# Products and ScalarE copies in place of VectorE transposes in the doubling inverse of a DeltaNet kernel

## Chip, cores and metric

The kernel runs on one core of one Trainium2 chip. The metric is the device time of one execution in microseconds. Each instruction goes to one of five engines: TensorE (PE; its weight loads are listed as PEld), VectorE (DVE), ScalarE (ACT), GpSimd (POOL) and SyncE (SP). Every engine takes its instructions in the order in which the program lists them. DMAs are issued here from SP's and ScalarE's queues, and a few at the start from GpSimd's.

## The reference

```python
q, k, v: (4, 8, 768, 48); beta: (4, 8, 768)           # float32
k_n = k / (norm(k) + 1e-06)
for t in range(768):
    y[:, :, t] = einsum('bhd,bhde->bhe', q[:, :, t], state)
    v_old = einsum('bhde,bhd->bhe', state, k_n[:, :, t])
    state += beta[:, :, t] * einsum('bhd,bhe->bhde', k_n[:, :, t], v[:, :, t] - v_old)
x = y as (3072, 384)
h = x @ w_in                                           # (3072, 2048)
out = (h * cos(h)) @ w_out                             # (3072, 384)
```

A delta-rule recurrence over 768 steps for 32 heads (4 batches, 8 heads), and behind it a feed-forward block whose activation is h cos h.

## The kernel before, in words

**The recurrence in chunks.** The 768 steps are cut into 24 units of C = 32 steps (`unit(n)`). For a unit, `turn` and `turn_out` put keys and queries with the head dimension on partitions, `gram` makes the products of keys with keys and queries, `gram_keys` scales the first, `gram_queries` masks the second. The unit's triangular system needs the inverse of a unit lower triangular 32x32 matrix for each of 32 heads. Then `state`, `right`, `solve`, `solve_out`, `update`, `update_out`, `within` and `features` go through the recurrence: `update_out(n)` changes the state that `state(n+1)` reads, so these are a chain from unit to unit. `features_out` writes the unit's share of the feed-forward input, `x_ffn`.

**Three ways to the inverse.** From unit 4 on the inverse is made on GpSimd by substitution (`invert`, lines 856 and 863), between two trips through DRAM (`gram_put`, `gram_get`, `put`, `get`). Units 2 and 3 (pair 1) invert halves of 16, partly on VectorE (tasks `inv 1 x`), and put them together with `solve_half`, `half_out`, `between`, `between_out`. Units 0 and 1 are inverted by doubling, without DRAM, and this is what is changed.

**Doubling.** `double_first` masks the scaled gram (line 691) and transposes it (701). `double_rest` builds identity minus the masked matrix (706) and masks the block off the diagonal (691 again). Then six levels follow, each for both head parities (`par`) and both units, 24 tasks `("double", n, level, par)`:

```python
LEVELS = [
    (LEFT, TURNED, 1), (SQUARE, SUM, 2), (LEFT, TURNED, 2),
    (SQUARE, SUM, 1), (OFF, TURNED, 1), (LEFT, SUM, 1),
]
```

An entry names the tile that is loaded as weights, the first tile that streams, and how many tiles stream side by side. Line 736 issues eight matmuls per task. Results are taken from PSUM by a ScalarE copy (744), a VectorE transpose (752), and a VectorE addition (756). At levels 0, 1 and 2 a transpose of the product is needed, at level 3 one of the sum (749).

**Norms.** `norms_square` (ScalarE, 554) and `norms_sum` (VectorE, 559) give the squared norm of the keys, `norms_root` (GpSimd, 571) its root. `scale` runs five small VectorE operations: plus 1e-6 (582), square (584), reciprocal (585), times beta (587), spread (590). It runs 14 times in all, four of them for units 0 to 3.

**Weights.** w_in and w_out arrive as 28 pieces in a wider format. Each piece goes through `narrow_load` (DMA), `narrow_split` on ScalarE (lines 525 and 529), `narrow_shift` on VectorE (533) and `narrow_add` on GpSimd (537). `hidden(p, f)` for k-th quarter of columns needs the pieces up to 3(k + 1); the output products need the pieces from 12 on.

**Feed-forward.** The first two pairs of units use plain products (`hidden`, line 1076; the very first also plain `output`, 1274), later ones products with fewer multiplications (`layer`, 1250; `product`, 1332), with sums of inputs and results on VectorE and GpSimd.

**Order.** `add(key, engine, cost, emit, deps, ...)` lists a task with what it depends on. The tasks are numbered in the order of these calls, and `Order.LINE` gives the order in which they are emitted, found beforehand and written out as numbers. `Order.OTHER` lists the tasks that take their second choice: DMAs on ScalarE's queue in place of SP's, sums on GpSimd in place of VectorE or the other way round. Among the tasks are 56 calls of `keep_warm`, placed by `LINE` like the others: a matmul of 128x256 on a constant tile (line 492, two rows in the profile), which nobody reads. A call emits nothing once the first output product has been emitted.

Of the kernel before, what the change touches and what calls it, by code (L numbers as in the profile page):

```python
# [59 lines left out]
class Order:  # L60

    OTHER = {
        ('gram_put', 2), ('q', 3), ('gram_get', 1), ('inv', 1, 0), ('put', 1), ('gram_put',
        4), ('gram_put', 5), ('v', 7), ('v', 8), ('v', 9), ('blocks', 11, 1), ('gram_put',
        11), ('put', 5), ('v', 13), ('put', 6), ('gram_put', 15), ('gram_get', 7), ('get',
        15), ('v', 16), ('blocks', 16, 0), ('blocks', 16, 1), ('gram_put', 16), ('blocks',
        18, 1), ('k', 19), ('blocks', 19, 0), ('gram_get', 9), ('get', 19), ('gram_put',
        20), ('v', 21), ('gram_put', 21), ('put', 10), ('gram_put', 22), ('v', 23),
        ('gram_put', 23), ('gram_get', 11), ('right', 4, 4), ('left', 1, 1, 0), ('left', 1,
        3, 0), ('left', 1, 3, 1), ('store', 1, 0), ('x_sum', 2, 'd'), ('x_sum', 2, 'n'),  # L70
        ('x_sum', 2, 'm'), ('x_sum', 2, 'e'), ('x_sum', 2, 'k'), ('x_sum', 2, 'g'),
        ('x_sum', 2, 'i'), ('x_sum', 2, 'l'), ('x_sum', 2, 'f'), ('x_sum', 2, 'b0'),
        ('left', 2, 4, 1), ('left', 2, 3, 1), ('x_sum', 3, 'd'), ('x_sum', 3, 'n'),
        ('x_sum', 3, 'm'), ('x_sum', 3, 'e'), ('x_sum', 3, 'k'), ('x_sum', 3, 'g'),
        ('x_sum', 3, 'i'), ('x_sum', 3, 'l'), ('x_sum', 3, 'h'), ('x_sum', 3, 'b0'),
        ('left', 3, 4, 1), ('left', 3, 3, 1), ('x_sum', 4, 'd'), ('x_sum', 4, 'm'),
        ('x_sum', 4, 'g'), ('x_sum', 4, 'i'), ('left', 4, 3, 0), ('left', 4, 3, 1),
        ('store', 4, 0), ('x_sum', 5, 'd'), ('x_sum', 5, 'e'), ('x_sum', 5, 'l'), ('x_sum',
        5, 'h'), ('x_sum', 5, 'b0'), ('left', 5, 2, 0), ('left', 5, 4, 1), ('left', 5, 3,
        0), ('left', 5, 3, 1), ('store', 5, 0), ('x_sum', 6, 'd'), ('x_sum', 6, 'g'),  # L80
        ('x_sum', 6, 'l'), ('x_sum', 6, 'f'), ('x_sum', 6, 'b0'), ('left', 6, 1, 0),
        ('left', 6, 4, 0), ('store', 6, 1), ('x_sum', 7, 'd'), ('x_sum', 7, 'm'), ('x_sum',
        7, 'g'), ('x_sum', 7, 'i'), ('x_sum', 7, 'f'), ('x_sum', 7, 'h'), ('x_sum', 7,
        'b0'), ('left', 7, 4, 0), ('left', 7, 4, 1), ('left', 7, 3, 1), ('x_sum', 8, 'd'),
        ('x_sum', 8, 'm'), ('x_sum', 8, 'e'), ('x_sum', 8, 'k'), ('x_sum', 8, 'g'),
        ('x_sum', 8, 'l'), ('left', 8, 3, 0), ('store', 8, 0), ('store', 8, 1), ('x_sum', 9,
        'd'), ('x_sum', 9, 'm'), ('x_sum', 9, 'e'), ('x_sum', 9, 'k'), ('x_sum', 9, 'i'),
        ('x_sum', 9, 'l'), ('x_sum', 9, 'b0'), ('left', 9, 1, 0), ('left', 9, 2, 0),
        ('left', 9, 1, 1), ('left', 9, 3, 0), ('store', 9, 0), ('x_sum', 10, 'k'), ('x_sum',
        10, 'i'), ('x_sum', 10, 'l'), ('x_sum', 10, 'h'), ('x_sum', 10, 'b0'), ('left', 10,  # L90
        1, 0), ('left', 10, 1, 1), ('left', 10, 4, 1), ('left', 10, 3, 0), ('left', 10, 3,
        1), ('store', 10, 0), ('x_sum', 11, 'd'), ('x_sum', 11, 'e'), ('x_sum', 11, 'k'),
        ('x_sum', 11, 'g'), ('x_sum', 11, 'f'), ('left', 11, 1, 0), ('left', 11, 2, 0),
        ('left', 11, 1, 1), ('left', 11, 3, 0), ('left', 11, 3, 1), ('store', 11, 1),
        ('store_right', 11), ('weights', 5), ('weights', 7), ('weights', 15), ('weights',
        16), ('weights', 18), ('weights', 20), ('weights', 22), ('weights', 23), ('weights',
        25), ('weights', 27)
# [142 lines left out]
def kernel(  # L240
# [84 lines left out]
    def half(i):  # L325
        return slice(DP * i, DP * i + DP)
# [1599 lines left out]
```

## Time and profile before

| | us |
|---|---|
| median of 3 runs | 639.41 (638.9 to 640.19) |
| the profiled execution | 643.63 |
| its span, first to last instruction | 641.8 |
| granted TensorE clock, mean | 0.992 |

The profile is of one execution. Its page lists for each engine the busy time, the share of the span and the instructions, and then the span in 40 slices of 16 us, where a digit is the busy share in tenths; PEclk is the clock that TensorE was granted. A granted clock below 1 makes matmuls longer. The trace behind the page answers for a stretch: the busy time of each engine in it, the instructions in order of time with what ended the idle time before them, and the chain of waits, which goes back from the last instruction to whatever released it.

The work of units 0 and 1 lies in the first 75 us. Some starting points: the first `turn` product at 6.78, the first `gram` at 10.29, the first doubling product at 15.06, `solve` of unit 0 at 48.48, the first `hidden` product at 60.43, `solve` of unit 1 at 65.44.

### The profile page before, as it was taken

To read this page: it belongs to the slowest core of one execution; us is meant where nothing else is said; L and a number is where in the kernel's file an instruction comes from. 1 tells how busy PE (TensorE), PEld (TensorE's weight loads), DVE (VectorE), ACT (ScalarE), POOL (GpSimd) and SP (SyncE) were. 2 spreads that over 40 slices of the span, in tenths; PEclk is the share of its full clock that TensorE was granted. 3 is DMA by queue.
4 is the path that set the end of the run, shared out by engine and by line. 5 is a ranking of instruction groups with operands and counts; after the bars stand their busy time and mean duration, and the time that the engine had idled before them with its cause. 6 is when DMAs were issued, how large, how long until landed. Compare 5 with 4: busy or idle time off the path is not lost.

```text
span 641.8 us, 24181 instructions
## 1 busy us (share of the span) xinstructions
PE 621.0 (97%) x10176; PEld 577.7 (90%) x10176; DVE 495.8 (77%) x1025; ACT 297.6 (46%) x528; POOL 435.2 (68%) x780
## 2 busy tenths in 40 slices
PE   5999989999999999999999999999999999999997
PEld 4867877997899999999999999999999999999997
DVE  5786746788899999887888898888888786656682
ACT  3447645563334454643642544643643553545440
POOL 5337787778778788888789887886883883112231
PEclk9899989999999999999999999999999999999999
DMA  9869565563551454435436235243304102000000
GB/s 186 213 141 236 103 163 121 117 119 54 101 81 22 92 91 70 88 69 83 79 64 103 49 68 101 51 65 66 72 4 82 41 2 42 19 2 26 1 25 25
DMA packets 209380, 50.36 MB, mean 78 GB/s; under 512 B 200920, under 2 KB 204280, under 8 KB 209272
## 3 DMA queue, kind: packets, MB, share of 16 engines
q1 hardware_dynamic: 161896, 35.03, 29.2%
q10 hardware_dynamic: 47072, 13.25, 9.9%
q8 instruction: 80, 1.31, 0.8%
q0 software_dynamic: 304, 0.54, 0.4%
q14 instruction: 28, 0.23, 0.1%
HBM read 38.55 MB, written 10.22 MB: 76 GB/s over the span
## 4 chain that ended last, share of the span: by engine, by line
PE 88%; DVE 5%; DMA 3%; issue 1%; ACT 1%; SPq 0%; POOL 0%; ACTq 0%; DVEq 0%
PE p_out L1332 28%; PE p_h L1250 27%; PE p_h L1076 7%; PE p_kq L907 4%; PE p_out L1274 3%; PE p_s L1004 3%; PE p_g L652 3%; PE p_kq L1034 3%; PE p_u L979 2%; PE p_h L736 2%; PE p_out L492 2%; PE p_h L1332 2%; PE p_z L1055 1%; DMA kp<-in_k_dram 1%; DMA out_dram<-o 1%
## 5 line engine op out<-in xcount | busy, mean ns | idle before, releaser
L856 POOL TENSOR_TENSOR part<-z,gb 128x126 f32<-128x126 f32 (+23 forms) x321 | 142.5, 444 | 42.8 <-DMA gb<-g_dr 13.7
L863 POOL TENSOR_TENSOR z<-z,part 128x126 f32<-128x126 f32 (+23 forms) x321 | 146.0, 455 | 25.2
L1332 PE MATMUL p_out<-w_out,g_ffn 128*128 128x192 f32 x672 | 121.8, 328 | 1.3 <-ACT o L1371 0.7
L1332 PEld LDWEIGHTS p_out<-w_out,g_ffn 128*128 128x128 f32 x672 | 107.7, 190 | 2.5 <-ACT o L1371 0.8
L1129 ACT ACTIVATE turns<-turns,halfpi 128x512 f32<-128x512 f32 x96 | 68.0, 719 | 55.7 <-DVE turns L1120 43.0
L1332 PE MATMUL p_out<-w_sum,g_ffn 128*128 128x192 f32 x496 | 89.7, 329 | 0.2 <-DVE o L1384 0.2
L1250 PE MATMUL p_h<-x_sum,w_in 128*128 128x128 f32 x640 | 84.0, 277 | 0.0
L1332 PEld LDWEIGHTS p_out<-w_sum,g_ffn 128*128 128x128 f32 x496 | 79.6, 190 | 1.2 <-issue 0.4
L1113 ACT ACTIVATE turns<-g_ffn,quarter_turn 128x512 int32<-128x512 f32 x70 | 49.8, 719 | 66.1 <-DVE g_ffn L1267 23.5
L1250 PEld LDWEIGHTS p_h<-x_sum,w_in 128*128 128x128 f32 x640 | 78.8, 192 | 1.2
L1267 DVE TENSOR_TENSOR g_ffn<-g_ffn,p_h 128x512 f32<-128x512 f32 x80 | 54.2, 680 | 16.1 <-PE p_h L1250 15.4
L1120 DVE SCALAR_TENSOR_TENSOR turns<-g_ffn,turns 128x512 f32<-128x512 f32 x70 | 55.2, 795 | 13.2 <-ACT turns L1113 13.0
L1047 ACT COPY y<-p_kq 32x384 f32<-32x384 f32 x96 | 45.2, 470 | 34.1 <-PE p_kq L1034 25.3
L1132 DVE TENSOR_TENSOR g_ffn<-turns,g_ffn 128x512 f32<-128x512 f32 x70 | 51.9, 750 | 4.1 <-ACT turns L1129 4.0
L1250 PE MATMUL p_h<-x_sum,in_sum 128*128 128x128 f32 x400 | 53.0, 277 | 0.4 <-DVE g_ffn L1267 0.4
L571 POOL TENSOR_TENSOR knrm<-ksum,halves 128x16 f32<-128x16 f32 (+1 forms) x14 | 36.3, 2596 | 24.9 <-DVE ksum L559 24.9
L1250 PEld LDWEIGHTS p_h<-x_sum,in_sum 128*128 128x128 f32 x400 | 49.6, 192 | 1.5 <-DVE g_ffn L1267 0.7
L1384 DVE SCALAR_TENSOR_TENSOR o<-p_out,o 128x192 f32<-128x192 f32 x74 | 25.1, 351 | 29.5 <-PE p_out L1332 28.4
L1076 PE MATMUL p_h<-x_ffn,w_in 128*128 128x128 f32 x384 | 47.4, 283 | 0.0
L1076 PEld LDWEIGHTS p_h<-x_ffn,w_in 128*128 128x128 f32 x384 | 45.7, 198 | 1.2
L1250 PE MATMUL p_h<-x_ffn,w_in 128*128 128x128 f32 x320 | 42.4, 277 | 0.0
L1348 POOL TENSOR_TENSOR g_ffn<-g_ffn,g_ffn 128x512 f32<-128x512 f32 x18 | 25.8, 1442 | 23.1 <-PE p_out L1332 19.3
(163 smaller groups left out, 1072.1 us busy)
## 6 DMA issues: line engine op xcount, KB each, us to landing
g_ffn<-in_moe_w_in_dram SPq DMA_DIRECT2D x10, 512.0 KB
gb<-g_dr SPq DMA_DIRECT2D x14, 256.0 KB
vp<-in_v_dram SPq DMA_DIRECT2D x68, 48.0 KB
g_ffn<-in_moe_w_out_dram SPq DMA_DIRECT2D x8, 384.0 KB
g_ffn<-in_moe_w_out_dram ACTq DMA_DIRECT2D x8, 384.0 KB
kp<-in_k_dram SPq DMA_DIRECT2D x120, 24.0 KB
out_dram<-o SPq DMA_DIRECT2D x14, 192.0 KB
zt<-z_dr SPq DMA_DIRECT2D x72, 32.0 KB
```

What stands on the lines that cost most here:

```text
L571: nc.gpsimd.tensor_tensor(out=scales[m][2][:, part], in0=sums[m, part.start][:, 0:n], in1=halves[:, 0:n], op=ALU.pow,)
L856: eng.tensor_tensor(out=part, in0=z[:, 0:rows, j, None].to_broadcast(shape), in1=a[:, j, None, j + 1 :].to_broadcast(shape), op=ALU.mult,)
L863: eng.tensor_tensor(out=behind, in0=behind, in1=part, op=ALU.subtract)
L1047: nc.scalar.copy(by_parity(y[quarter(b)]), p_kq[quarter(b ^ 1), :, b % 2])
L1076: nc.tensor.matmul(p_h[:, i], w_in[:, t, (4 * k + i) * 128 : (4 * k + i + 1) * 128], xts[p][:, t, unit * 128 : (unit + 1) * 128], start=(i ...
L1113: nc.scalar.activation(turns[p, f], hidden_of(p, f), AF.Identity, bias=quarter_turn, scale=TURN)
L1120: nc.vector.scalar_tensor_tensor(out=r, in0=hidden_of(p, f), scalar=TURN, in1=t, op0=ALU.mult, op1=ALU.subtract,)
L1129: nc.scalar.activation(r, r, AF.Sin, bias=halfpi, scale=2.0 * math.pi)
L1132: nc.vector.tensor_tensor(out=place(p, f), in0=step_of(rests.pop((p, f)), f), in1=step_of(hidden_of(p, f), f), op=ALU.mult,)
L1250: nc.tensor.matmul(p_h[:, e], in_block(*w)[:, e], x_of(p, b), start=new and e == 0, stop=True, skip_group_check=True,)
L1267: nc.vector.tensor_tensor(out=part_of(p, to), in0=part_of(p, one), in1=part_of(p, two), op=op)
L1332: nc.tensor.matmul(p_o, left(p, part, a)[:, e % 4], right(e, b), start=(e == 0), stop=(e == FT // 2 - 1), skip_group_check=True,)
```

## The change

The `scale` of the norms is split: 1e-6 and the square go to two ScalarE activations with a bias tile (`norms_near`, a task `near` of its own between `norms` and `scale`). The off-diagonal mask becomes a GpSimd task `double_off`, which level 4 waits for. Level 0 makes the product and, by exchanging the two operands, its transpose; level 2 does the same with its first half. The transposes of levels 0 and 2 become ScalarE copies; that of level 1 stays.

```diff
-    tiny = const.tile([128, 2, H], FP, name="tiny")
+    tiny = const.tile([128, 1], FP, name="tiny")
...
+    def norms_near(m, part):
+        knrm = scales[m][2][:, part]
+        krec = krecs[m, part.start] = work.tile([128, 2, H], FP, name="krec")[
+            :, 0 : part.stop - part.start
+        ]
+        nc.scalar.activation(krec, knrm, AF.Square, bias=tiny)
+        nc.scalar.activation(knrm, knrm, AF.Identity, bias=tiny)
...
     def scale(m, part):
-        nc.vector.tensor_tensor(out=knrm, in0=knrm, in1=tiny[:, 0:n], op=ALU.add)
-        krec = work.tile([128, 2, H], FP, name="krec")[:, 0:n]
-        nc.vector.tensor_tensor(out=krec, in0=knrm, in1=knrm, op=ALU.mult)
+        krec = krecs.pop((m, part.start))
         nc.vector.reciprocal(krec, krec)
...
-        masked(n, OFF, far_block)
+    def double_off(n):
+        masked(n, OFF, far_block, nc.gpsimd)
...
     LEVELS = [
-        (LEFT, TURNED, 1), (SQUARE, SUM, 2), (LEFT, TURNED, 2),
-        (SQUARE, SUM, 1), (OFF, TURNED, 1), (LEFT, SUM, 1),
+        [(LEFT, TURNED, 1, 0), (TURNED, LEFT, 1, 1)], [(SQUARE, SUM, 2, 0)],
+        [(TURNED, LEFT, 1, 0), (LEFT, SUM, 1, 1)], [(SQUARE, SUM, 1, 0)],
+        [(OFF, TURNED, 1, 0)], [(LEFT, SUM, 1, 0)],
     ]
-    TURNS = {0: (SQUARE, 0), 1: (LEFT, 1), 2: (SQUARE, 0)}
+    TURNS = {0: (SQUARE, 1), 1: (LEFT, 1), 2: (SQUARE, 0)}
...
-            nc.vector.transpose(m[:, to, par], p_ds[n, par][:, at])
+            if level == 1:
+                nc.vector.transpose(m[:, to, par], p_ds[n, par][:, at])
+            else:
+                nc.scalar.copy(m[:, to, par], p_ds[n, par][:, at])
...
+        add(("double_off", n), "POOL", 1.1, lambda: double_off(n), [("double_first", n)])
...
-                deps = last[par] + ([("double_rest", n)] if level == 1 else [])
+                deps = last[par] + {1: [("double_rest", n)], 4: [("double_off", n)]}.get(level, [])
...
+            add(("near", m, a), "ACT", 0.5, lambda: norms_near(m, part), [("norms", m, a)])
```

`LINE` and `OTHER` are new as well. On TensorE, by tasks (W3 stands for three calls of `keep_warm`; `double n level par`; the other numbers are the unit, or pair and column group):

```
before  turn 0, W2, gram 0, turn 1, double 0 0 1, 0 0 0, gram 1, W1, double 0 1 0, 1 0 0, W2,
        double 0 1 1, 1 1 0, W3, 0 2 0, W2, 0 2 1, 1 0 1, turn 2, W2, double 1 1 1, turn 3,
        double 0 3 0, 0 3 1, W1, gram 2, W1, double 1 2 0, W2, 0 4 1, W2, gram 3, double 0 4 0, W2,
        1 2 1, 0 5 0, 0 5 1, turn 4, W1, solve 0
after   turn 0, W2, gram 0, W1, turn 1, double 0 0 1, 0 0 0, gram 1, W3, double 0 1 1, 0 1 0, W1,
        1 0 0, 0 2 1, turn 2, W2, double 0 3 1, turn 3, double 1 0 1, 0 2 0, 1 1 0, gram 2, W4,
        double 0 3 0, W2, 0 4 1, 1 1 1, W1, 0 4 0, gram 3, double 0 5 1, 0 5 0, W3, turn 4,
        double 1 2 0, solve 0
```

```
before  hidden 0 4, solve_half 2, W1, between 2, W1, solve 2, hidden 0 6, update 2, W1, within 2, gram 6,
        hidden 0 8, features 2, state 3, turn 7, hidden 0 10, solve_half 3, between 3, solve 3,
        out 0 0 0, hidden 0 12, update 3
after   hidden 0 4, W2, state 2, W1, features 1, W1, turn 6, W1, solve_half 2, hidden 0 6, between 2,
        solve 2, out 0 0 0, update 2, within 2, gram 6, hidden 0 8, state 3, turn 7, hidden 0 10,
        solve_half 3, between 3, solve 3, hidden 0 12, features 2, update 3
```

On ScalarE after the first `turn_out`: `near`, square of unit 1, `turn_out 1`, `near`, copy of level 0, the four DMAs of k(3), square of unit 2, the new copy that replaces the first transpose, copy of level 0, a weight load, two activations of weight piece 1, the second such copy, two of piece 0, copy of level 1. On SP the keys of unit 2 now come ahead of the weights, whose first piece goes to ScalarE's queue. From `layer 5 17` on, in the second half of the kernel, TensorE's order is as before.

More of the change, by code (lines that the diff above doesn't have):

```diff
@@ L62 @@
     OTHER = {
[L63 to L92, printed above, removed]
+        ('gram_put', 2), ('k', 3), ('inv', 1, 0), ('inv', 1, 1), ('v', 4), ('put', 2),
@@ new lines @@
+        ('gram_get', 3), ('get', 8), ('put', 4), ('v', 10), ('blocks', 11, 0), ('gram_put',
+        11), ('gram_get', 5), ('v', 12), ('blocks', 12, 0), ('blocks', 12, 1), ('v', 13),
+        ('blocks', 13, 1), ('gram_put', 13), ('put', 6), ('blocks', 14, 1), ('blocks', 15,
+        1), ('put', 7), ('get', 15), ('v', 17), ('k', 19), ('blocks', 19, 0), ('gram_get',
+        9), ('get', 19), ('gram_put', 20), ('v', 21), ('gram_put', 21), ('put', 10),
+        ('gram_put', 22), ('v', 23), ('gram_put', 23), ('gram_get', 11), ('store', 0, 0),
@@ new lines @@
+        ('store', 0, 1), ('right', 3, 4), ('right', 2, 6), ('left', 1, 4, 1), ('left', 1, 3,
+        0), ('left', 1, 3, 1), ('store', 1, 0), ('x_sum', 2, 'd'), ('x_sum', 2, 'm'),
+        ('x_sum', 2, 'e'), ('x_sum', 2, 'k'), ('x_sum', 2, 'g'), ('x_sum', 2, 'l'),
+        ('x_sum', 2, 'f'), ('x_sum', 2, 'b0'), ('left', 2, 3, 0), ('left', 2, 3, 1),
+        ('x_sum', 3, 'd'), ('x_sum', 3, 'n'), ('x_sum', 3, 'm'), ('x_sum', 3, 'e'),
+        ('x_sum', 3, 'k'), ('x_sum', 3, 'i'), ('x_sum', 3, 'l'), ('x_sum', 3, 'b0'),
@@ new lines @@
+        ('left', 3, 4, 0), ('left', 3, 4, 1), ('left', 3, 3, 0), ('left', 3, 3, 1),
+        ('store', 3, 0), ('x_sum', 4, 'n'), ('x_sum', 4, 'i'), ('x_sum', 4, 'f'), ('x_sum',
+        4, 'h'), ('x_sum', 4, 'b0'), ('left', 4, 4, 1), ('left', 4, 3, 0), ('store', 4, 0),
+        ('x_sum', 5, 'd'), ('x_sum', 5, 'e'), ('x_sum', 5, 'h'), ('x_sum', 5, 'b0'),
+        ('left', 5, 2, 0), ('left', 5, 4, 1), ('left', 5, 3, 0), ('left', 5, 3, 1),
+        ('store', 5, 0), ('x_sum', 6, 'd'), ('x_sum', 6, 'g'), ('x_sum', 6, 'l'), ('x_sum',
@@ new lines @@
+        6, 'f'), ('x_sum', 6, 'b0'), ('left', 6, 1, 0), ('left', 6, 4, 0), ('store', 6, 1),
+        ('x_sum', 7, 'd'), ('x_sum', 7, 'm'), ('x_sum', 7, 'g'), ('x_sum', 7, 'i'),
+        ('x_sum', 7, 'f'), ('x_sum', 7, 'h'), ('x_sum', 7, 'b0'), ('left', 7, 4, 0),
+        ('left', 7, 4, 1), ('left', 7, 3, 1), ('x_sum', 8, 'd'), ('x_sum', 8, 'm'),
+        ('x_sum', 8, 'e'), ('x_sum', 8, 'k'), ('x_sum', 8, 'g'), ('x_sum', 8, 'l'), ('left',
+        8, 3, 0), ('store', 8, 0), ('store', 8, 1), ('x_sum', 9, 'd'), ('x_sum', 9, 'm'),
@@ new lines @@
+        ('x_sum', 9, 'e'), ('x_sum', 9, 'k'), ('x_sum', 9, 'i'), ('x_sum', 9, 'l'),
+        ('x_sum', 9, 'b0'), ('left', 9, 1, 0), ('left', 9, 2, 0), ('left', 9, 1, 1),
+        ('left', 9, 3, 0), ('store', 9, 0), ('x_sum', 10, 'k'), ('x_sum', 10, 'i'),
+        ('x_sum', 10, 'l'), ('x_sum', 10, 'h'), ('x_sum', 10, 'b0'), ('left', 10, 1, 0),
+        ('left', 10, 1, 1), ('left', 10, 4, 1), ('left', 10, 3, 0), ('left', 10, 3, 1),
+        ('store', 10, 0), ('x_sum', 11, 'd'), ('x_sum', 11, 'e'), ('x_sum', 11, 'k'),
@@ L576, in norms_root @@
         )
+    def norms_near(m, part):
[5 more added lines that the diff above has]
+        nc.scalar.activation(knrm, knrm, AF.Identity, bias=tiny)
+    krecs = {}
     def scale(m, part):
         n = part.stop - part.start
-        bs, bz, knrm = (t[:, part] for t in scales[m])
-        nc.vector.tensor_tensor(out=knrm, in0=knrm, in1=tiny[:, 0:n], op=ALU.add)
-        krec = work.tile([128, 2, H], FP, name="krec")[:, 0:n]
-        nc.vector.tensor_tensor(out=krec, in0=knrm, in1=knrm, op=ALU.mult)
+        bs, bz = (t[:, part] for t in scales[m][0:2])
+        krec = krecs.pop((m, part.start))
         nc.vector.reciprocal(krec, krec)
@@ L687, with masked @@
     TURNED, SUM, NEXT, LEFT, SQUARE, OFF = range(POWERS // 2)
-    def masked(n, to, mask):
+    def masked(n, to, mask, eng=nc.vector):
         m = power(n)
-        nc.vector.tensor_tensor(
+        eng.tensor_tensor(
             out=m[:, to].rearrange("p a j (o i) -> p (a j o) i", i=C),
@@ L732, in double @@
         ).rearrange("p (x j i) -> p x j i", x=2, i=2 * C)
-        one, two, wide = LEVELS[level]
-        for j in range(NP):
-            for i in range(2):
-                nc.tensor.matmul(
-                    p[half(i), 0:wide, j],
-                    m[half(i), one, par, j],
-                    m[half(i), two : two + wide, par, j],
-                )
+        for one, two, wide, at in LEVELS[level]:
+            for j in range(NP):
+                for i in range(2):
+                    nc.tensor.matmul(
+                        p[half(i), at : at + wide, j],
+                        m[half(i), one, par, j],
+                        m[half(i), two : two + wide, par, j],
+                    )
     def double_copy(n, level, par):
@@ L1460, in doubling @@
                     then = ("double_" + what, n, level, par)
-                    add(then, "ACT" if what == "copy" else "DVE", 0.35,
+                    on_scalar = what == "copy" or what == "turn" and level != 1
+                    add(then, "ACT" if on_scalar else "DVE", 0.35,
                         lambda emit=emit, level=level, par=par: emit(n, level, par),
@@ L1500, in unit @@
                 makes=[] if a else [("scales", ("scales", m))], uses=[("ksum", m, a)])
-            add(("scale", m, a), "DVE", 1.1, lambda: scale(m, part),
-                [("norms", m, a), ("beta",) if n < PLAIN_TURNS else ("beta_home",)])
+            add(("near", m, a), "ACT", 0.5, lambda: norms_near(m, part), [("norms", m, a)])
+            add(("scale", m, a), "DVE", 0.65, lambda: scale(m, part),
+                [("near", m, a), ("beta",) if n < PLAIN_TURNS else ("beta_home",)])
         scaled = ("scale", m, a if n < 4 else 0)
```

5 lines of the change are left out of this document (2 added, 3 removed), and 201 rows, old and new, of the table LINE.

## The prediction

> **What bounds the kernel now.** I read the page first: busy times and slices.
>
> ```profile
> PE 621.0 (97%) x10176; PEld 577.7 (90%) x10176; DVE 495.8 (77%) x1025; ACT 297.6 (46%) x528; POOL 435.2 (68%) x780
> ...
> PE   5999989999999999999999999999999999999997
> ...
> PEclk9899989999999999999999999999999999999999
> ```
>
> TensorE is the bound, and the only slices with room are the first ones. So a change in the doubling, which all lies ahead of 65 us, can pay only by letting TensorE get to its long full stretch sooner. Next the busy time by stage (columns: PE, PEld, DVE, ACT, POOL, clock, DMA share, GB/s). I cut at 15 us (first doubling product) and at 111 us: there `update` of unit 3 starts (first L1004 of it at 110.93), and up to there both orders have issued the same useful products, so all that the start gains or loses is in when this point comes.
>
> ```profile
> 15.00:48.00 33.00, 31.48 (x542) 25.23 (x542) 27.95 (x74) 14.75 (x31) 10.43 (x7) 0.90 0.76 177
> 48.00:80.00 32.00, 29.44 (x676) 25.66 (x679) 21.67 (x54) 21.57 (x43) 24.69 (x35) 1.00 0.74 170
> 80.00:111.00 31.00, 27.47 (x729) 23.75 (x719) 16.93 (x37) 16.54 (x32) 25.30 (x52) 0.94 0.57 145
> 111.00:642.00 531.00, 524.93 (x8160) 497.17 (x8159) 421.26 (x838) 239.28 (x414) 366.16 (x671) 1.00 0.34 60
> ```
>
> TensorE idles 1.5 + 2.6 + 3.5 = 7.6 us between 15 and 111. Behind 111 it idles 6.1 us in 531, and nearly 4 of that is the last store, so there is nothing to win there. But its busy time is not all work: the same windows for L492 alone show 58 matmul rows, that is 29 calls of keep_warm (two rows each; fillers below), 18.2 us. Those stand in the line whether TensorE would otherwise wait or not. The chain of waits shows what sets the doubling's pace; in 28 to 39 us it is VectorE:
>
> ```profile
> 31.59 0.35 DVE in_sum L752
> 31.94 1.40 DVE w_in L533
> 33.34 1.18 DVE knrm L582
> ...
> 34.55 1.23 DVE krec L584
> ...
> 37.68 0.34 DVE in_sum L756
> ...
> 38.06 0.97 PE p_h L736 x13
> ```
>
> From 29.4 to 38.0 every piece is VectorE's, and TensorE's longest wait for it in the doubling, 1.2 us, ends at 38.06. The change takes L582 and L584 and two thirds of L752 off this engine.
>
> **The parts.**
>
> *Products for transposes.* Level 0 issues 16 matmuls instead of 8 for each of four unit-parity pairs. Each matmul is two rows, so 64 rows are added. From the timeline:
>
> ```profile
> 15.06 1.97 PE L736 MATMUL p_h<-in_sum 64*64 64x64 f32 x32 [2.88 <-DVE knrm L582]
> ...
> 33.65 1.15 PE L736 MATMUL p_h<-in_sum 64*64 64x64 f32 x32
> ...
> 40.14 0.68 PE L736 MATMUL p_h<-in_sum 64*64 64x64 f32 x16
> ```
>
> Sixteen such rows take 0.61 us in the chain (40.21 and 42.67), so 4 x 0.61 = 2.4. Unit 0's half of them stands at the clock of 0.5 granted from 14.9 to about 20.7 us: 32 rows took 1.97 there and 1.15 later, another 0.8. Together **+3.2 us**. Level 2 costs nothing: 16 rows 128 wide (1.09) become 32 rows 64 wide (1.10 to 1.15).
>
> *ScalarE copies.* Eight transposes of 0.44 us leave VectorE (3.5), eight copies of 0.37 (row L744) join ScalarE, which is busy 14.75 of 33 us. The copy itself is shorter. What counts is what is ahead of it: ScalarE takes its list in order, with two activations per weight piece (L525 0.68, L529 0.66) and DMA issues between. Before, the copy after the product that ended at 23.86 ran at 25.35, since four q issues held ScalarE's queue from 22.48 to 25.25. After, the four issues of k(3) stand between the first level-0 copy and its turn. Per copy that is 0 to 1.5 us; most of it lies under the three and four keep_warm calls that follow (0.53 each), so I take 0 and keep the rest for a rival.
>
> *The norms.* Two VectorE operations (0.17 each, 0.4 us with their starts) become two ScalarE ones (nearest row: the 128x1 activation L459, 0.20) 14 times. Behind the doubling this is covered by TensorE's full stretch: 0. At the start ScalarE waits for the power on GpSimd, which ends at 11.63, with the second square and the second turn_out queued behind it. The reciprocal still starts near 12.06; but the second sum (0.55) now comes ahead of gram_keys. The first product moves from 15.06 to about 15.5: **+0.4**. The filler moved ahead of turn(1) lies in the idle 12.2 to 15.06.
>
> *The mask.* Two operations of 0.69 leave VectorE for GpSimd (nearest row of its size and kind, L537: 1.35). Level 4 needs it, more than 15 us later: 0 for its length. But GpSimd's work costs VectorE something:
>
> ```profile
> 31.77 3.98 POOL L537 TENSOR_TENSOR w_in<-w_in,g_ffn 128x512 uint32<-128x512 uint32 x3
> ...
> 33.27 1.25 DVE L582 TENSOR_TENSOR knrm<-knrm,tiny 128x8 f32<-128x8 f32 x1
> ```
>
> L582's median is 0.17; here, and in L584 after it, it lasts until the GpSimd operation beside it ends. [...] I count neither in the sum: only TensorE's waits are in it.
>
> *Fillers.* The new order has 29 keep_warm calls ahead of the first output product instead of 31, and 26 instead of 29 behind the first doubling product. Four rows take 1.06 in the chain, so one is 0.53: **-1.6**.
>
> *Waits of TensorE* (7.6, of which one gap of 2.1 is taken below; 5.5 left). Bounds: all go (-5.5), or new ones replace them (0 or, by the rival, worse). The 1.2 at 38 us was VectorE's and goes. Also, hidden(0,6) now stands between solve_half(2) and between(2), where TensorE waited 0.43 for half_out, and solve_out(2) is covered by the first output product. I take **-2.2**, nearest to these rows.
>
> *The gap at 84 us.*
>
> ```profile
> 85.77 0.28 PE L973 MATMUL p_u<-g_ffn,w_sum 32*32 32x48 f32 x5 [2.07 <-issue]
> ...
> 85.98 4.57 PE L1076 MATMUL p_h<-x_ffn,w_in 128*128 128x128 f32 x24
> ...
> 93.53 2.94 PE L1076 MATMUL p_h<-x_ffn,w_in 128*128 128x128 f32 x24
> ```
>
> Within one group of products TensorE stops 2.07 us for nothing that the profile shows, and the next 24 products run at a granted clock near 0.55: 4.5 in the chain, not 2.7. Together 3.9. The profiled execution took 643.63 (span 641.8, 1.8 around it), 4.2 above the median of 639.41, so the gap may belong to this execution alone (0), or it comes in all and the new order, with 24 long products between the three short groups, avoids it (-3.9). I see nothing nearer to either end and take the middle, **-1.9**.
>
> *Order and queues.* On SP k(2) goes ahead of the first weight piece, which moves to ScalarE's queue with k(3); q(3), both puts of units 4 and 5, and the put and get of pair 1 move to SP. Weight pieces 0 to 2 land about 2 us later, but the first hidden product starts at 60 us and needs only three. Inversion of pair 2 was done on GpSimd between weight adds; now the adds come first. Its reader, solve(4), had no wait. Behind 111 us the same products stand in another order up to feed-forward pair 5: 0, bounds -1 and +3.
>
> **Sum**: 3.2 + 0.4 - 1.6 - 2.2 - 1.9 = -2.1. On the profiled execution 641.5; on the median 639.41 - 2.1 = **637.3**.
>
> **Rivals.**
>
> *Slower: ScalarE's order becomes the bound.* Place: levels 0 to 3 of unit 0, where copies and the norms' pair wait behind weight activations (1.35 a piece) and k(3)'s issues (2.8 by the q row). Level 1 of unit 0 needs a copy behind k(3) and two pieces; level 3 one behind turn_out(2) (1.05); the scale of pair 1 waits for a norms pair further back, and behind that scale on VectorE stands the last transpose of level 1. It decides once such a wait outlasts the fillers ahead (1.6 and 1.1 us). Three places at 0.5 to 1.7 each: 3.5. With the waits and the gap not won back: 3.2 + 0.4 - 1.6 + 3.5 less 2.2 = +3.3, 642.7; with half of it 641. For it: the 25.35 row. Against: ScalarE is under half busy.
>
> *No change.* Products and start (+3.6) are paid by fillers and waits (-3.8), and the gap is not in the timed runs: 639.2. The same comes out if the masks on GpSimd hold VectorE so that it isn't relieved.
>
> *The clock stays up.* Half clock followed a wait of 2.9 us (12.2 to 15.06) and one of 2.07. The new filler shortens the first to about 2.5. If that is too short for the throttle, 5.8 us at 0.5 become 2.9: 637.3 - 2.9 = 634.4. [...]
>
> **Chances.** Forecast 0.42; slower by ScalarE 0.30; no change 0.19; clock 0.09. The measurement tells 0.2% (1.3 us) from no change: faster 0.49, within 0.20, slower 0.31. The likeliest case alone spans 635.0 (gap in full) to 638.1; with the rivals and bounds the range is 634.4 to 642.7.
>
> **What would show it.** Four transposes in `double_turn` at levels 0 to 2 where L752 has 12; the first doubling product near 15.5; no VectorE run of 8 us in the chain from 29 to 38; unit 3's L1004 before 109. Wrong if TensorE waits on ScalarE copies for over 1 us at levels 1 to 3, if solve(0) (48.48 now) starts past 50, or if new waits show behind 111 us.

## The result, and the profile after

The changed kernel takes 646.81 us (median of 4 runs, 645.99 to 649.27); the kernel before, beside it, 639.80 (638.9 to 640.39). The ratio is 1.0113, with a 95% interval of 1.0090 to 1.0137: slower by some 7 us, where 637.3 was forecast and the range ended at 642.7. The profiled execution took 649.27 (span 647.5, clock 0.989). The lines of its page that answer to those of before:

```profile
PE 622.4 (96%) x10300; PEld 581.2 (90%) x10300; DVE 486.2 (75%) x988; ACT 306.8 (47%) x564; POOL 436.5 (67%) x781
...
PE   6899898999999999999999999999999999999997
...
PEclk8998999999999999999999999999999999999999
```

The edit did what it says: VectorE lost 9.6 us of work, ScalarE gained 9.2, TensorE has 124 rows more. TensorE is still the bound, and the slices with room are still the early ones. The stages (columns as before: PE, PEld, DVE, ACT, POOL, clock, DMA share, GB/s):

```profile
15.00:48.00 33.00, 29.72 (x602) 25.20 (x602) 19.92 (x55) 18.89 (x44) 12.21 (x13) 0.90 0.77 196
48.00:80.00 32.00, 28.48 (x635) 25.96 (x635) 24.08 (x56) 18.56 (x40) 20.83 (x26) 0.95 0.66 159
80.00:111.00 31.00, 26.62 (x785) 22.62 (x784) 16.45 (x34) 17.67 (x34) 25.07 (x56) 1.00 0.53 111
111.00:647.00 536.00, 528.38 (x8198) 500.30 (x8187) 418.33 (x823) 246.55 (x437) 370.82 (x676) 1.00 0.35 62
```

Between 15 and 111 us TensorE idles 3.3 + 3.5 + 4.4 = 11.2 us, where it idled 7.6 (10.5 in a second profile of the changed kernel, e11 below). VectorE has 8 us less to do between 15 and 48 (4 less in e11), and TensorE waits longer: VectorE was relieved and nothing came sooner. `update` of unit 3, which was to start before 109 us, starts at 115.5, and at 111.05 in e11. In the chain of waits, the stretch ahead of a wait of TensorE that both profiles have:

```profile
46.74 1.21 DVE g L786
...
49.44 0.36 DVE w_sum L766
49.80 0.83 DVE ksum L560
50.63 0.34 DVE w_sum L772
...
50.99 0.35 ACT w_sum L768
51.34 0.30 ACT w_sum L757
...
51.69 2.15 PE p_h L749 x46
```

L768 is the ScalarE copy that replaces a transpose, L757 an older copy of the doubling. The next products of the doubling wait for L757, and L757 stands behind L768 on ScalarE. TensorE waits 1.3 us for it, and in e11 the same:

```profile
48.00 1.56 PE L749 MATMUL p_h<-w_sum 64*64 64x64 f32 x46 [1.33 <-ACT w_sum L757]
```

One wait of the first profile does not come in every execution. The second turn of unit 3, which reads q(3), waited for a DMA (the row names one of v), and the products behind it ran at a granted clock of 0.5 (from 32 to 35 us):

```profile
31.68 0.86 PE L628 MATMUL p_t<-consts,qp 128*128 128x128 f32 x4 [1.96 <-DMA vp<-in_v_dram]
32.46 1.98 PE L749 MATMUL p_h<-w_sum 64*64 64x64 f32 x32
```

In e11 (span 642.3) that turn ran at 29.54 without a wait, and the median was about the same (646.19).

### The profile page after: what moved, and what is told of

Read it like the earlier page. It is cut to its first block, busy times and chain, and to the rows that moved or that the text cites. A ratio compares the mean times of both kernels' runs of the same rounds, so it can differ in the third digit from the quotient of the medians.

```text
span 647.5 us, 24421 instructions
## 1 busy us (share of the span) xinstructions
PE 622.4 (96%) x10300; PEld 581.2 (90%) x10300; DVE 486.2 (75%) x988; ACT 306.8 (47%) x564; POOL 436.5 (67%) x781
## 3 DMA queue, kind: packets, MB, share of 16 engines
q8 instruction: 81, 1.33, 0.9%
## 4 chain that ended last, share of the span: by engine, by line
PE 73%; POOL 8%; DMA 6%; DVE 6%; SPq 3%; issue 3%; ACT 1%; DVEq 0%; POOLq 0%; ACTq 0%
PE p_out L1348 27%; PE p_h L1266 24%; PE p_h L1092 5%; POOL z L879 4%; POOL part L872 4%; PE p_kq L923 3%; PE p_s L1020 3%; PE p_kq L1050 2%; PE p_u L995 2%; DMA qp<-in_q_dram 2%; PE p_g L661 2%; PE p_h L1348 2%; DMA kp<-in_k_dram 2%; PE p_h L749 1%; DMA gb<-g_dr 1%
## 5 line engine op out<-in xcount | busy, mean ns | idle before, releaser
L872 POOL TENSOR_TENSOR part<-z,gb 128x126 f32<-128x126 f32 (+24 forms) x317 | 137.1, 433 | 45.9 <-DMA gb<-g_dr 17.2
L879 POOL TENSOR_TENSOR z<-z,part 128x126 f32<-128x126 f32 (+24 forms) x317 | 144.5, 456 | 24.8
L1063 ACT COPY y<-p_kq 32x384 f32<-32x384 f32 x96 | 45.1, 470 | 19.6 <-PE p_kq L1050 14.5
L1092 PEld LDWEIGHTS p_h<-x_ffn,w_in 128*128 128x128 f32 x384 | 44.1, 192 | 2.0 <-issue 0.9
L1364 POOL TENSOR_TENSOR g_ffn<-g_ffn,g_ffn 128x512 f32<-128x512 f32 x19 | 28.1, 1481 | 23.2 <-PE p_out L1348 19.4
```

The lines of the kernel that those rows point to most:

```text
L872: eng.tensor_tensor(out=part, in0=z[:, 0:rows, j, None].to_broadcast(shape), in1=a[:, j, None, j + 1 :].to_broadcast(shape), op=ALU.mult,)
L879: eng.tensor_tensor(out=behind, in0=behind, in1=part, op=ALU.subtract)
L1063: nc.scalar.copy(by_parity(y[quarter(b)]), p_kq[quarter(b ^ 1), :, b % 2])
L1092: nc.tensor.matmul(p_h[:, i], w_in[:, t, (4 * k + i) * 128 : (4 * k + i + 1) * 128], xts[p][:, t, unit * 128 : (unit + 1) * 128], start=(i ...
```

## The experiments

After the result two theories stood: A, the new order carries the loss; B, the edit does, whatever the order. Each ratio is to the kernel before, run beside it; one per mille is 0.64 us. "Products" means the further products of levels 0 and 2 together with the copies that replace the transposes.

| run | order | parts of the edit | ratio (95%) |
|---|---|---|---|
| e1_products_old_order | old | products | 1.0019 (1.0006 to 1.0033) |
| e2_norms_mask_old_order | old | norms, mask | 1.0040 (1.0024 to 1.0055) |
| e3_all_old_order | old | all | 1.0073 (1.0054 to 1.0092) |
| e4_order_alone | new | none | 0.9991 (0.9972 to 1.0009) |
| e5_order_norms_mask | new | norms, mask | 1.0054 (1.0031 to 1.0077) |
| e6_order_products | new | products | 1.0053 (1.0036 to 1.0069) |
| e7_order_products_mask | new | products, mask | 1.0063 (1.0042 to 1.0084) |
| e8_order_products_norms | new | products, norms | 1.0090 (1.0052 to 1.0128) |
| e9_vload_on_sync | new | all, v(4) issued by SP | 1.0079 (1.0055 to 1.0104) |
| e10_products_unused | new | products' TensorE work alone | 1.0028 (1.0005 to 1.0050) |
| e11_after_again | new | all | 1.0108 (1.0066 to 1.0150) |
| e12_norms_vload_on_sync | new | norms, v(4) issued by SP | 1.0027 (1.0009 to 1.0045) |
| e13_first_norms_scalar | new | first four norms pairs | 1.0015 (0.9996 to 1.0033) |
| e14_later_norms_scalar | new | later ten, v(4) issued by SP | 1.0001 (0.9988 to 1.0015) |
| e15_mask_alone | new | mask | 0.9998 (0.9981 to 1.0016) |
| e16_copies_on_vector | new | products, copies on VectorE | 1.0016 (0.9998 to 1.0034) |
| e17_three_mended | new | all but three places | 1.0019 (1.0008 to 1.0030) |
| e18_copies_on_scalar_again | new | products | 1.0050 (1.0032 to 1.0067) |

### The order or the edit

**Products in the old order (e1)**

> The kernel before, in its own order, with the products and ScalarE copies alone (levels 0 and 2); norms and mask as before. Theory A, the new order carries the loss (new waits behind VectorE, GpSimd and the late q of unit 3): the products add 3.2 us of TensorE work to the line and take 1 to 3 us of VectorE waits out of it, so 638.5 to 642, and the first update of unit 3 at 110 to 113 us instead of 110.9. Theory B, the edit itself carries it (more products at half clock, copies queued on ScalarE): 643 to 647 and update of unit 3 near 115, as in the kernel after.

```diff
+        [(LEFT, TURNED, 1, 0), (TURNED, LEFT, 1, 1)], [(SQUARE, SUM, 2, 0)],
+        [(TURNED, LEFT, 1, 0), (LEFT, SUM, 1, 1)], [(SQUARE, SUM, 1, 0)],
...
+                nc.scalar.copy(m[:, to, par], p_ds[n, par][:, at])
```

Slower by 1.2 us.

**Norms and mask in the old order (e2)**

> The kernel before, in its own order, with the norms' two operations on ScalarE and the mask on GpSimd, products and transposes as before. Theory A: VectorE's stretch of 29 to 38 us loses L582 and L584 (2.4 us there), so 637.5 to 640.5. Theory B says little: 639 to 641. If ScalarE's list holds the second pair's scale up, 641 to 643.

```diff
+        nc.scalar.activation(krec, knrm, AF.Square, bias=tiny)
+        nc.scalar.activation(knrm, knrm, AF.Identity, bias=tiny)
...
+        masked(n, OFF, far_block, nc.gpsimd)
```

Slower by 2.6 us, and here one sees the first form of what follows. ScalarE, and then the first doubling product on TensorE, in the timelines of e2:

```profile
11.79 0.66 ACT L525 ACTIVATE w_in<-g_ffn 128x512 f32<-128x512 f32 x1 [1.21 <-DMA g_ffn<-in_moe_w_in_dram]
12.35 0.64 ACT L529 ACTIVATE g_ffn<-g_ffn 128x512 uint32<-128x512 uint32 x1
12.89 0.28 ACT L583 ACTIVATE krec<-knrm,tiny 128x8 f32<-128x8 f32 x1
```

```profile
16.21 1.97 PE L736 MATMUL p_h<-in_sum 64*64 64x64 f32 x32 [4.51 <-DVE in_sum L701]
```

The norms' square (L583) stands in ScalarE's list behind the split of a weight piece, which waits until 11.79 for its DMA. The first doubling product then starts at 16.21 instead of 15.06.

**All of it in the old order (e3)**

> All three edits in the order of before (the norms' activations where the scale stood, the mask where it stood). Theory A: 638 to 641.5, since only the order differs from the kernel after. Theory B: 644 to 648, as after.

Both edits above together: 4.7 us slower, where the two alone give 1.2 + 2.6. The intervals are too wide to tell 4.7 from that sum.

**The order alone (e4)**

> The new order alone: order, queues and engine choices of the kernel after, with the operations of before on VectorE at the places of the new tasks. Theory A: at least the kernel after's time, 645 to 650 (VectorE has its old work as well). Theory B: 639 to 642.

```diff
-        nc.scalar.activation(krec, knrm, AF.Square, bias=tiny)
-        nc.scalar.activation(knrm, knrm, AF.Identity, bias=tiny)
+        nc.vector.tensor_tensor(out=knrm, in0=knrm, in1=tiny[:, 0:n], op=ALU.add)
+        nc.vector.tensor_tensor(out=krec, in0=knrm, in1=knrm, op=ALU.mult)
```

(and the old levels, transposes and mask.) No difference that can be told: theory A falls. Theory B does not hold as it was put either: the same edit costs 4.7 us in the old order (e3) and, from here to the changed kernel, 7.8 in the new one. And the gains that I booked on the order are not there. Its stages from 15 to 111:

```profile
15.00:48.00 33.00, 31.88 (x644) 26.67 (x646) 29.68 (x79) 19.86 (x40) 13.48 (x11) 0.95 0.87 219
48.00:80.00 32.00, 28.68 (x624) 24.80 (x621) 25.26 (x60) 19.29 (x39) 23.02 (x29) 1.00 0.66 157
80.00:111.00 31.00, 27.53 (x775) 24.16 (x774) 17.48 (x36) 15.97 (x31) 24.02 (x63) 1.00 0.56 120
```

TensorE idles 1.1 + 3.3 + 3.5 = 7.9 us, as much as before (7.6).

### Which part of the edit

Two parts of the edit stand against each other here: the products with their copies, and the norms with the mask.

> The changed kernel with the old level table: all nine turns VectorE transposes again, no further products; the norms' two operations on ScalarE, the mask on GpSimd and the new order stay. The order alone gave 638.91, all of it 646.81; this tells which part of the edit costs those 7.9. Theory P (the doubling products and the copies that turn into them on ScalarE carry it): this run stands near the order alone, 639 to 640.5. [...] Theory X (neither by itself; the two together push level 0 far enough that unit 3's turn meets the DMA of q(3), and the clock falls behind that wait): 639.5 to 641.5, with no wait above 1 us in front of unit 3's turn.

> The changed kernel with the norms' two operations and the mask on VectorE again; the products, the ScalarE copies and the new order stay. Theory P: 645 to 647, nearly all of the loss. [...] Theory X: 640 to 642; solve of unit 0 starts between 43.2 (order alone) and 49.2 (changed kernel).

> The changed kernel with the norms' two operations on VectorE again; the products, the copies, the mask on GpSimd and the new order stay. [...] By theory X it falls if the wait in front of unit 3's turn goes, by 3 to 4 us with its half-clock stretch.

> The changed kernel with the mask on VectorE again; the products, the copies, the norms on ScalarE and the new order stay. [...] Theory P: 645.5 to 647, a mask that is off the chain changes nothing. Theory X: no more than 1 us below the changed kernel.

Four mixtures in the new order; the old parts are put back as in the diffs above, reversed. Neither theory P nor theory X held. The products cost 4.0 us (e6 against e4), norms and mask 4.0 (e5 against e4), and all together 7.8 (the changed kernel against e4): the parts add up. The mask is small in these differences (1.0063 against 1.0053), the norms look larger (1.0090 against 1.0053), though these two intervals overlap.

### Norms behind DMA issues

In the trace of e8 a reason shows at 92 us. OTHER puts the four DMA issues of v(4) on ScalarE's queue, and a norms pair stands behind them (issues from 92.64 for 1.84 us, the square at 94.53).

> The changed kernel with the four DMA issues of v(4) on SyncE instead of ScalarE's queue; nothing else moves. In the changed kernel's trace these issues hold ScalarE from 94.57 to 96.42 and the norms' Square runs behind them at 96.46; VectorE's reciprocal, and behind it the sum L1028 that gram 6 waits for (1.5 us), stand behind that Square. Theory Q (ScalarE's in-order queue: the norms' pair stands behind DMA issues): the Square follows the GpSimd root by under 0.5 us, the reciprocal runs 1.5 to 3 us earlier, gram 6's wait falls to about 0.3, and the time falls by 1.5 to 2.5 us against the changed kernel. Theory R (the hop between engines costs by itself, 0.3 and 0.3 us of activations with their semaphores, wherever they stand): no more than 0.5 us is gained.

```diff
-        ... ('inv', 1, 1), ('v', 4), ('put', 2),
+        ... ('inv', 1, 1), ('put', 2),
```

> The changed kernel once more, unaltered, on the chip of the other three: 1.009 to 1.0137 of before. What is open is whether the 2.0 us in front of unit 3's second turn, where q(3) landed at 31.65, belongs to the kernel or to the one profile: it was in none of the four mixtures, which all share the order of DMA issues. If the kernel makes it, it is there again; if the landing of that DMA varies, it is not, and the time does not change by it.

The changed kernel again (e11), ScalarE's timeline, then VectorE's:

```profile
90.50 1.84 ACTq L397 DMA_DIRECT2D vp<-in_v_dram  x4
92.39 0.31 ACT L584 ACTIVATE krec<-knrm,tiny 128x16 f32<-128x16 f32 x1 [1.23 <-DMA vp<-in_v_dram]
```

```profile
92.73 0.25 DVE L594 RECIPROCAL krec<-krec 128x16 f32<-128x16 f32 x1 [1.75 <-ACT krec L584]
...
93.57 0.94 DVE L1028 TENSOR_TENSOR st<-st,p_s 128x768 f32<-128x768 f32 x1
```

In e9 the same reciprocal:

```profile
92.09 0.25 DVE L594 RECIPROCAL krec<-krec 128x16 f32<-128x16 f32 x1 [0.41 <-ACT krec L584]
```

And TensorE's waits in e11, then in e9:

```profile
PE p_g L661 <- DVE st L1028: 1.5, 1, 1.5
```

```profile
PE p_g L661 <- DVE st L1028: 0.3, 1, 0.3
```

ScalarE issues for 1.84 us; the square comes behind that; VectorE's reciprocal waits 1.75 for it; the sum of the state (L1028) comes behind the reciprocal; gram 6 waits for the sum. With the issues on SP the reciprocal waits 0.41 and the gram 0.3. The time falls from 1.0108 to 1.0079, by 1.9 us, of which this wait accounts for 1.2. The intervals overlap, but taking the same issues away without the products gives the same difference (e5 1.0054, e12 1.0027; e12 also has the mask back on VectorE, which by itself will turn out to move nothing):

> The order alone with the norms' two operations on ScalarE and v(4) issued by SyncE; transposes and mask on VectorE. Theory Q: 0.997 to 1.001 of before, as the order alone, since with v(4) out of ScalarE's queue the pair costs VectorE less and TensorE nothing. Theory R: 1.002 to 1.0045, what the norms added in the mixtures (1.009 against 1.0053).

```diff
-        ... ('inv', 1, 1), ('v', 4), ('put', 2),
+        ... ('inv', 1, 1), ('put', 2),
```

(on e4 with the norms on ScalarE.) 1.0027 lies above the order alone, as theory R had it, so the issues seem not to be the norms' whole cost. Splitting the fourteen pairs narrows down where the rest is:

> The order alone with only the first four of the norms' pairs (128x8, units 0 to 3) on ScalarE; the other ten, the mask and the transposes on VectorE. If the loss of the norms is made at the start, where the pair stands among ScalarE's first copies and DMA issues: 1.001 to 1.004 of before. If it is made later (reciprocals that wait for ScalarE): as the order alone, 0.998 to 1.0005.

> The order alone with the ten later pairs (128x16) on ScalarE and v(4) issued by SyncE; the first four on VectorE. If the loss is made by the later pairs, 1.001 to 1.004; if it is made at the start or by v(4) alone, 0.998 to 1.0005.

```diff
+        if n == 1:      # e14: n == 2
+            nc.scalar.activation(krec, knrm, AF.Square, bias=tiny[:, 0, 0:1])
+            nc.scalar.activation(knrm, knrm, AF.Identity, bias=tiny[:, 0, 0:1])
+        else:
+            nc.vector.tensor_tensor(out=knrm, in0=knrm, in1=tiny[:, 0:n], op=ALU.add)
+            nc.vector.tensor_tensor(out=krec, in0=knrm, in1=knrm, op=ALU.mult)
```

The ten later pairs cost nothing that can be told once v(4) is out of their way. What is left is with the first four, but 1.0015 is not certainly above 1 and its interval overlaps that of e14: taken alone that run is inconclusive. The mask:

> The order alone with the mask on GpSimd (1.27 us there). If the mask costs what the difference of the mixtures gave, 1.0 to 1.001 of before. If taking 0.35 us per mask off VectorE's chain helps, 0.997 to 0.999. More than 1.002 would say that GpSimd's mask is itself late for level 4, which no wait in the traces shows.

```diff
+        masked(n, OFF, far_block, nc.gpsimd)
```

Neither gain nor loss.

### Products, or where their copies run

> The order alone, with the further doubling products of levels 0 and 2 issued as in the changed kernel, but level 0's second product is read by nobody: all turns stay VectorE transposes and no copy moves to ScalarE. The order alone was 0.9991 of before, with the products and ScalarE copies 1.0053, so these two cost 0.6%, some 4 us. Theory W (TensorE's work is the cost): 1.004 to 1.0055, since the products of the doubling stand one after another on TensorE: 22.0 against 19.6 us of p_h rows make 2.4 us, and the clock some more. Theory S (the copies on ScalarE make the next level late): 0.9995 to 1.002, with the wait of 1.4 us for ScalarE's copy ahead of the products near 48 gone. Both at once: 1.003.

```diff
-        (LEFT, TURNED, 1), (SQUARE, SUM, 2), (LEFT, TURNED, 2),
+        [(LEFT, TURNED, 1, 0), (TURNED, LEFT, 1, 1)], [(SQUARE, SUM, 2, 0)],
+        [(LEFT, TURNED, 1, 0), (LEFT, SUM, 1, 1)], [(SQUARE, SUM, 1, 0)],
```

The second product of level 0 is issued and left out of the result, and the transposes stay. TensorE's work alone costs 1.0028 - 0.9991, 2.4 us, which is what the rows of e6 and e4 say: 22.0 us of p_h rows (L750) against 19.6 (L749), both at a granted clock of 0.95 between 15 and 48 us. In e10's own profile, at 1.00, they are 20.8.

> New order with the products, where the copies of levels 0 and 2 that stand for the transposes are made by VectorE; norms and mask on VectorE. If the copies' place on ScalarE is what makes the next level wait, this is as the products that nobody reads, 1.001 to 1.004, and the wait of 1.4 us for ScalarE near 48 is gone. If the products' work on TensorE and the chain are all, 1.004 to 1.0065, as with the copies on ScalarE.

> New order, products with their copies on ScalarE, norms and mask on VectorE, a second time. If the copies' place on ScalarE costs what the first reading gave: 1.004 to 1.0065, against 1.0016 with the copies on VectorE. If that difference was the chip's: 1.001 to 1.003.

```diff
-                nc.scalar.copy(m[:, to, par], p_ds[n, par][:, at])
+                nc.vector.tensor_copy(m[:, to, par], p_ds[n, par][:, at])
...
-                    on_scalar = what == "copy" or what == "turn" and level != 1
+                    on_scalar = what == "copy"
```

(From e18 to e16.) The same eight copies of 128x256 take 0.37 us on ScalarE and 0.41 on VectorE, and on VectorE the kernel is 2.2 us faster (1.0016 against 1.0050). What ScalarE does at 47 us in e18, then in e16:

```profile
47.51 0.37 ACT L769 COPY w_sum<-p_h 128x256 f32<-128x256 f32 x1 [1.88 <-DVE w_sum L773]
...
47.78 0.38 ACT L758 COPY w_sum<-p_h 128x256 f32<-128x256 f32 x1
...
50.64 0.35 ACT L769 COPY w_sum<-p_h 128x256 f32<-128x256 f32 x1
```

```profile
45.89 0.37 ACT L758 COPY w_sum<-p_h 128x256 f32<-128x256 f32 x1 [0.65 <-DVE w_sum L767]
```

In e18 the first new copy (L769) waits 1.88 us for an addition on VectorE (L773, 47.03 to 47.43), and the older copy L758 waits behind it. In e16 L758 follows the transpose L767 at once; in e18 that transpose had ended at 46.3 (45.83 + 0.43). The second new copy stands behind four activations of weight pieces until 50.64, and now VectorE waits, as its timeline in e18 shows:

```profile
47.03 0.40 DVE L773 TENSOR_TENSOR w_sum<-w_sum,p_h 128x256 f32<-128x256 f32 x1
...
51.02 0.75 DVE L773 TENSOR_TENSOR w_sum<-w_sum,p_h 128x256 f32<-128x256 f32 x2 [2.67 <-ACT w_sum L769]
```

Each engine stands once in front of the other. TensorE pays for both. Its timeline in e18, then in e16, where neither wait exists:

```profile
48.21 1.56 PE L750 MATMUL p_h<-w_sum 64*64 64x64 f32 x46 [1.39 <-ACT w_sum L758]
...
56.62 0.68 PE L750 MATMUL p_h<-w_sum 64*64 64x64 f32 x16 [1.17 <-DVE w_sum L763]
```

```profile
46.32 1.77 PE L750 MATMUL p_h<-w_sum 64*64 64x64 f32 x48
...
54.35 0.68 PE L750 MATMUL p_h<-w_sum 64*64 64x64 f32 x16
```

1.39 + 1.17 = 2.6 us of waits against 2.2 measured. The new order has a part in it: in the old one, with the same copies on ScalarE (e1, e3), neither wait is there, TensorE waits 0.7 us for one such copy of unit 0, and the products with their copies cost 1.2 us (e1) where they cost 3.8 to 4.0 in the new one (e18 and e6 against e4). The kernel's text shows what the two share: at level 2 copy and addition read the two halves of one PSUM tile, `p_ds[n, par]`, and in each pair the one that comes later waits for the earlier one. That the shared tile is the reason was not tested.

### Are these all?

> The changed kernel with three things undone: the copies of levels 0 and 2 made by VectorE, v(4) issued by SyncE, the first four norms pairs on VectorE. The products, the mask on GpSimd, the ten later norms pairs on ScalarE and the new order stay. If the three places carry the loss, what is left is the products' own work: 1.001 to 1.0035 of before (the copies on VectorE alone gave 1.0016, the later norms and the mask each nothing). If something else in the changed kernel carries a part, it stays above 1.005.

The changed kernel with the edits of e9 and e16 and the pairs of e14: 1.0019. So the three places together carry the loss beyond the products' own work: 1.0108 to 1.0019, 5.7 us. In steps from the repeat of the changed kernel, 1.0108: v(4)'s issues 0.0029 (1.9 us), the copies on ScalarE 0.0034 (2.2), and down to 1.0019 another 0.0026 (1.7), which falls to the first four norms pairs by subtraction (0.0024 by e13 against e4, 0.0014 by e13 against e14). Each single step is uncertain by 1.4 to 3 us; the sum of the three is clear of that. What is left above the order alone, 0.0028 (1.8 us), is the products. No version was measurably faster than the kernel before.

## Why the prediction was wrong, step by step

**The products** (+3.2): right in kind, perhaps over-sized. Alone they cost 2.4 (e10), with copies on VectorE 1.6 (e16), and the intervals of these differences still hold 3.2. The 0.8 for half clock on unit 0 does not come in every execution: in the profile of e10 the first 64 rows ran in 2.08 us (granted clock 1.00), in that of e6 in 3.44 (0.50 from 16 to 18 us).

**ScalarE copies**: this step failed. "What counts is what is ahead of it" was the right question; "so I take 0 and keep the rest for a rival" was the wrong answer. They cost 2.2 us in the new order. I looked only at unit 0 and at the keep_warm calls behind its products; the costly copies are two of unit 1's, around `solve` 0, where the new order has no such call. I also asked only what is ahead of a copy, and not who stands behind it: an older copy, and VectorE's additions. The row on which the step rests held the hint. The copy that ran at 25.35 in the profile of before is listed with VectorE's addition as what released it, not with the DMA issues:

```profile
25.35 0.37 ACT L744 COPY in_sum<-p_h 128x256 f32<-128x256 f32 x1 [1.11 <-DVE in_sum L756]
```

That addition ended at 25.11, the issues at 25.25, so the row does not tell which of the two held the copy; I had taken it for the issues alone.

**The norms**: "Behind the doubling this is covered by TensorE's full stretch: 0" failed. One pair in ten was not covered, because v(4)'s issues, which the new OTHER puts on ScalarE, stand right ahead of it: 1.9 us. I had weighed k(3)'s issues, not v(4)'s, and had not read ScalarE's new list between 75 and 111 us at all. The start (+0.4) was under-sized if the first pairs carry the 1.7 us that the differences leave them; the first product came at 15.29 (15.00 in e11; 15.04 in e4), so hardly any of it is made there. The wait for a DMA ahead of the turn that reads q(3) (1.96 in the first profile of the changed kernel) stands in the profiles of e5, e12, e13, e14 and e15 too (0.6, 2.75, 1.4, 0.9 and 1.1 us), with the first pairs on ScalarE and without, and doesn't tell it. Two profiles point to a later place: `update` of unit 3 starts at 110.88 in e9, with the norms and the mask moved, and at 111.15 in e18, with both on VectorE,

```profile
110.88 0.89 PE L1020 MATMUL p_s<-u,kp 64*64 64x96 f32 x32 [0.57 <-ACT x_ffn L1079]
```

```profile
111.15 0.89 PE L1021 MATMUL p_s<-u,kp 64*64 64x96 f32 x32 [0.57 <-ACT x_ffn L1080]
```

and yet e9's span is 3.8 us longer (644.0 against 640.2). These are single executions, and where those 1.7 us arise stays open.

**The mask** (0): right (0.9998). With the two operations on GpSimd (1.27 and 1.38 us) and two of 0.69 gone from VectorE, the time did not move. In before, one L582 and the L584 after it took 1.25 and 1.22 us beside three L537 on GpSimd (31.77 to 35.75), against a median of 0.17. Why, and whether the masks on GpSimd do the same to VectorE, was not tested.

**Fillers, waits and the gap** (-1.6 - 2.2 - 1.9 = -5.7): failed. They hang on the order, and the order alone gives 0.0009 of the time, 0.6 us. Fewer fillers only became waits of TensorE (7.9 us of idle time without the gap, against 7.6 with it). The gap is real: e1, e2 and e3, all in the old order, show it too (1.64, 1.6 and 1.8 us), and in no profile of the new order does TensorE stop within those products for longer than 0.4. The half clock behind it (granted 0.5 from 86.2 to 89.6 us in before) is not steady: the next 24 products take 4.57 in before, e1 and e3, but in e2, whose profile lies 0.9 below its median, 2.94:

```profile
85.25 0.28 PE L973 MATMUL p_u<-g_ffn,w_sum 32*32 32x48 f32 x6 [1.58 <-issue]
85.46 2.94 PE L1076 MATMUL p_h<-x_ffn,w_in 128*128 128x128 f32 x24
```

So the new order does lose the gap and still gains only 0.6 us. What takes its place was not isolated; one part stands in ten of the sixteen profiles of the new order, where TensorE stops for 0.3 to 1.0 us within a later group, the p_kq products (L924 in e7: 1.00 at 98.84). And the profiled execution of before lay 4.2 above its median, and I took gains from it as if the median had them: e4's profile is 3.9 us shorter than that of before, its median 0.6.

So -2.1 became +7.0: products -1.4 against my term, copies +2.2, norms +3.2 (1.9 + 1.7 - 0.4), order +5.1, in all +9.1. The single terms carry the uncertainty of the steps above.

**The rivals.** "ScalarE's order becomes the bound" was the right one in its mechanism, and its sign was that of the result. Its places were off (levels 0 to 3 of unit 0 and k(3), where it was unit 1 and v(4)), its price was 3.5 where the three places cost 5.8, and its sum still held gains of the order: it takes off 2.2 for waits that its own sentence calls not won back. Without that it is +5.5, 644.9. "The clock stays up" did not happen in either profile of the changed kernel: the first 64 rows of the doubling took 3.42 us, and 3.49 in e11. (Its 5.8 us at 0.5 were 6.8: in before the granted clock stood at 0.5 from 14.5 to 21.3 us.) In e9, with the same products behind the same wait as in e11 (2.8 us), they took 2.08, at a granted clock of 1.00, so the length of that wait alone does not decide it. Of the signs named, TensorE's wait of over 1 us for ScalarE's copies came true; `solve` 0 past 50 did not (49.23, and 45.54 in the repeat); new waits behind 111 us did show, 1.3 for a state's zt and 1.5 in three waits for output sums, where before had 1.9 us of others. By themselves they don't carry the loss: e14 has 3.1 us of waits there and 1.0001. Whether they carry part of the open 1.7 no run tells.

**Two readings of the trace.** In e18 ScalarE starts L758 only behind L769, some 1.5 us after the end of the transpose that L758 follows at once in e16 (46.3 to 47.78). Four DMA issues took 1.84 us of ScalarE, and moving them gave 1.9 us of the kernel's time: the issue time itself was the loss (1.2 us of it as TensorE's wait), on the engine that had work behind it.

## What to carry to other kernels

When work moved to an engine that is half idle, its duration was the least of it here (0.37 us a copy against 0.41, and 2.2 us lost by the place): list what stands ahead of each moved instruction on that engine, DMA issues included, and what stands behind it and could have run sooner. The copies were shorter on ScalarE and cost more there, each engine standing once in front of the other (waits of 1.88 and 2.67 us in e18). And the place depends on the order around them (products with copies on ScalarE cost 1.2 us in the old order, 3.8 to 4.0 in the new): try such a move in the order in which it will stand. And take no gain from a single profile that lies above its own median; subtract that excess first.

## What the hardware showed that I had not expected

Half clock followed waits of 1.3 to 1.4 us in some executions and not in others. In the first profile of the changed kernel the granted clock fell to 0.5 between 52.4 and 55.8 us, behind the wait of 1.33 us that ended at 51.69; behind the same wait of 1.33 us in e11, the same kernel (granted clock 1.00 from 48 to 51 us), and behind that of 1.39 us at 48.21 in e18, the same 46 rows took 1.56 us against 2.15. So one profile of a stage this short says little of the clock in the next.
